# Linear attention and two dense layers on one core: two sums per slot accumulated on a bank copy, weight conversions in pairs

## The chip, the core and the metric

The kernel runs on one core of a Trainium2 chip. The metric is device time in microseconds (us). A core has a matrix engine (TensorE: PE in the rows, PEld for its weight loads), VectorE (DVE), ScalarE (ACT), GpSimd (POOL) and SyncE (SP, which here only issues transfers). Each engine works through its own instructions in order and waits for the others on semaphores. TensorE writes to PSUM, eight banks of 512 fp32 per partition; transfers run on 16 DMA engines.

## The reference

```python
kv = np.einsum('bhsd,bhse->bhde', k, v)          # attention: 8 x 8 heads, 576 tokens, 64 wide
out = np.einsum('bhsd,bhde->bhse', q, kv)
out = out / sqrt(mean(out * out) + 1e-06) * g_norm
x = out as [4608 tokens, 512]
h = x @ w_in;  g = max(h, 0) ** 2;  x = g @ w_out        # layer A: 512 -> 2048 -> 512
h = x @ w_in2; g = h * cos(h);      out = g @ w_out2     # layer B: the same sizes
```

The weights come as 64-bit floats. The kernel takes them as pairs of 32-bit words and makes fp32 of them with bit operations ("conversion"). Every large product is computed three times with a high and a low part of each operand (high·high, high·low, low·high), so that the sum has more bits than one pass gives.

## The kernel before

Up to about 498 us the kernel computes the attention, the first eight of layer A's 16 weight chunks, and converts weights. The rest, where the change lies, runs in 30 **slots**, made by `slots`: slot k is (layer m, token tile t, group q). Layer A (m = 0) has its other eight chunks left, two groups of four, for each of five token tiles (slots 0 to 9), layer B (m = 1) has four (slots 10 to 29). Tiles have halves of 512 tokens (t = 0, 1, 2) or 384 (t = 3, 4).

In a slot both matrix products are cut into 2 x 2 blocks, and the seven-product form of a 2 x 2 block product is used. The **first product** (`first_product`, L510) makes F0 to F6, 12 matmuls each, 84 a slot, into the bank pairs FA and FB by turns, in the order 0, 1, 3, 2, 5, 4, 6. Several of them accumulate on the one before in the same pair: F3 on F0, and so on. ScalarE and VectorE empty a pair in between: `keep` (L524, ScalarE, tiles m and u) copies F0 to SBUF, `add` (L530 for layer B, L534 for layer A, VectorE) adds F1 and the kept F0 to give block (0,0) of h, `last` (L539, ScalarE) takes F6. The four blocks of h then go through relu² (ScalarE, L543 and L547) or through h·cos h (`cos_1` to `cos_5`, L551 to L569, by turns ScalarE, VectorE, ScalarE, ScalarE, VectorE).

The **second product** of the slot runs 1.25 slots later (`LAG2`), between the matmuls of the first product of the next slots. In 25 slots (`seven`) it has the same form: `s_block` makes each of seven operands as a high part (ScalarE, L648, gh) and a low part (VectorE, L649, gl), some of them from differences of blocks (L631); `second_product` (L672) makes S0 to S6 into the pairs SA and SB by turns in the order `S_ORDER` = 0, 2, 3, 4, 5, 1, 6. `drain_product` adds each to sums in SBUF: on VectorE (L700), by a ScalarE copy to a tile `part` (L697) and a DMA that accumulates (L698), or by a ScalarE copy where it is the first (L692). The other five slots (q = 1 of layer A) use a plain product (`second`, L609; drained by VectorE, L622).

`run_slots` writes both products' matmuls in a fixed interleaving: one first-product matmul per step, 84 steps a slot, and the second product's spread evenly over the slot. Around them the list `jobs` sets when loads, copies and conversions are written, at a position in slots (`pos`; PH is a seventh of a slot). Weights for a product are loaded 2.7 sevenths ahead on SP's queue. A scheduler then orders each engine's instructions from this, so what stands in a queue is shown below from the built program.

While slots 1 to 7 run, the weights of layer B are converted: 16 units (`pair`), each a load of two 256 KB pieces into `raw`, the word operations (`words`, `value`, L119 to L133), four sums (L177), the high part (L189, ScalarE) and the low part (L191, VectorE), and two stores to `wi_d`. `raw` comes from the pool `conv` of two 4 KB buffers per partition, which the tiles `part` share later; the temporaries e and w come from the pool `t`, four of 2 KB.

## Time and profile before

| | us |
|---|---|
| median of 3 runs | 1583.31 (1581.37 to 1585.13) |
| the profiled execution | 1582.0 |
| its span on the core | 1580.2 |

The profile is that of one execution, 1.8 us longer than its span. TensorE's granted clock was 1.0 of full speed in every stretch. The share of the chain of work that ended last is PE 79%, DVE 8%, DMA 7%. Busy time of matmuls is modelled at their ends, so consecutive matmuls overlap in the rows: what one costs in a row of many is the distance between two starts, not its duration. Idle time of an engine that nobody waits for costs nothing.

### The profile page before, as it was taken

What the parts mean: (1) busy time and instruction counts of PE and PEld (TensorE: products, weight loads), DVE (VectorE), ACT (ScalarE), POOL (GpSimd) and SP (SyncE); (2) the same over time, 40 slices, a digit from 0 to 9 for tenths busy, and PEclk for the clock granted to TensorE, in tenths of its full rate; (3) what the DMA queues carried; (4) which work ended last, traced back from release to release, by engine and by line L of the source; (5) the groups of instructions that cost most, each with busy time, mean ns of one, the idle gap of its engine ahead of it and who ended that gap; (6) DMA issues with size and microseconds to landing.
All of it is one profiled execution on the core that took longest, in us unless ns stands there. A gap on an engine that the chain in (4) does not pass through costs nothing.

```text
span 1580.2 us, 24826 instructions
## 1 busy us (share of the span) xinstructions
PE 1547.6 (98%) x9164; PEld 1356.4 (86%) x9164; DVE 1256.6 (80%) x1714; ACT 1060.5 (67%) x1515; POOL 115.4 (7%) x125
## 2 busy tenths in 40 slices
PE   5999999999999999999999999999999999999998
PEld 3777777778887878888999899999999999999998
DVE  7988878788874888889847678967896788689777
ACT  5977777775443756565645667776777677777774
...
GB/s 317 282 158 243 263 235 278 240 202 207 185 219 256 298 271 336 302 335 330 374 281 291 246 213 270 266 277 246 267 260 291 230 260 290 277 363 314 284 351 164
DMA packets 236999, 425.53 MB, mean 269 GB/s; under 512 B 18512, under 2 KB 155216, under 8 KB 236880
## 3 DMA queue, kind: packets, MB, share of 16 engines
...
## 4 chain that ended last, share of the span: by engine, by line
PE 79%; DVE 8%; DMA 7%; issue 3%; ACT 2%; SPq 1%; POOL 0%; DVEq 0%; POOLq 0%; ACTq 0%
PE FA L510 14%; PE FB L510 14%; PE SA L672 12%; PE SB L672 12%; PE acc L422 10%; PE l L385 9%; PE SB L609 2%; PE SA L609 2%; DMA wi_d<-raw 2%; DMA raw<-in_wB 2%; PE o L385 1%; DMA sum<-part 1%; PE ss L385 1%; DMA ws_d<-raw 1%; DVE gl L649 1%
## 5 line engine op out<-in xcount | busy, mean ns | idle before, releaser
L510 PE MATMUL FA<-xh,wi 128*128 128x512 f32 (+1 forms) x840 | 306.0, 370 | 1.9 <-issue 1.0
L510 PE MATMUL FB<-xh,wi 128*128 128x512 f32 (+1 forms) x840 | 305.4, 370 | 0.0
L672 PE MATMUL SB<-ws,gh 128*128 128x256 f32 x1008 | 237.9, 280 | 1.1 <-ACT u L524 0.7
L672 PE MATMUL SA<-ws,gh 128*128 128x256 f32 x1008 | 237.9, 280 | 0.0
L672 PEld LDWEIGHTS SB<-ws,gh 128*128 128x128 f32 x1008 | 186.0, 188 | 14.4 <-ACT u L524 1.0
L672 PEld LDWEIGHTS SA<-ws,gh 128*128 128x128 f32 x1008 | 186.2, 188 | 13.2
L510 PEld LDWEIGHTS FA<-xh,wi 128*128 128x128 f32 x840 | 157.7, 188 | 12.1 <-issue 1.4
L510 PEld LDWEIGHTS FB<-xh,wi 128*128 128x128 f32 x840 | 157.8, 188 | 8.3 <-ACT h L539 0.3
L649 DVE TENSOR_TENSOR gl<-y,gh 128x1024 fp32r<-128x1024 f32 (+1 forms) x100 | 111.4, 1114 | 38.7 <-ACT gh L648 38.5
L672 PE MATMUL SA<-ws,gl 128*128 128x256 f32 x504 | 141.0, 280 | 1.1 <-DVE gl L649 1.1
L672 PE MATMUL SB<-ws,gl 128*128 128x256 f32 x504 | 141.2, 280 | 0.8 <-DVE gl L649 0.7
L698 POOL DMA_DIRECT2D sum<-part x71 | 60.3, 850 | 1093.4 <-ACT part L697 1078.6
L569 DVE SCALAR_TENSOR_TENSOR y<-y,h 128x1024 f32<-128x1024 f32 (+1 forms) x80 | 89.1, 1114 | 53.5 <-ACT y L565 53.2
L551 ACT ACTIVATE y<-h,zerob 128x1024 int32<-128x1024 f32 (+1 forms) x80 | 85.1, 1064 | 50.5 <-DVE h L530 50.5
L422 PE MATMUL acc<-gh,wh 128*128 128x512 f32 x288 | 113.6, 395 | 0.0
L422 PE MATMUL acc<-gl,wh 128*128 128x512 f32 x288 | 112.9, 392 | 0.0
L422 PE MATMUL acc<-gh,wl 128*128 128x512 f32 x288 | 112.6, 391 | 0.0
L510 PE MATMUL FA<-xl,wi 128*128 128x512 f32 (+1 forms) x300 | 111.0, 370 | 0.0
L510 PE MATMUL FB<-xl,wi 128*128 128x512 f32 (+1 forms) x300 | 110.9, 370 | 0.0
L672 PEld LDWEIGHTS SB<-ws,gl 128*128 128x128 f32 x504 | 94.7, 188 | 7.9 <-DVE gl L649 1.5
L672 PEld LDWEIGHTS SA<-ws,gl 128*128 128x128 f32 x504 | 94.7, 188 | 7.9 <-DVE gl L649 1.3
L385 PE MATMUL l<-xh,wh 128*128 128x512 f32 x240 | 96.6, 403 | 2.1 <-ACT xh L354 1.2
...
## 6 DMA issues: line engine op xcount, KB each, us to landing
wi<-wi_d SPq DMA_DIRECT2D x210, 512.0 KB, 7.0
ws<-ws_d SPq DMA_DIRECT2D x175, 512.0 KB, 5.9
sum<-part POOLq DMA_DIRECT2D x45, 512.0 KB, 7.6
kvld<-in_kv SPq DMA_DIRECT2D x32, 512.0 KB, 6.8
wi_d<-wh SPq DMA_DIRECT2D x24, 448.0 KB, 4.3
wi_d<-raw SPq DMA_DIRECT2D x24, 448.0 KB, 4.7
raw<-in_wA SPq DMA_DIRECT2D x20, 512.0 KB, 6.4
wo<-wo_d SPq DMA_DIRECT2D x20, 512.0 KB, 8.2
```

The source lines that it names most:

```text
L385: nc.tensor.matmul(ps, a[:, 0, cs], m[:], start=(c == 0 and k == 0), stop=(c == NKC - 1 and k == 2))
L422: nc.tensor.matmul(o, a[:, cs], m[:], start=(f == 0 and n == 0), stop=(f == NH - 1 and n == 2), skip_group_check=True)
L510: nc.tensor.matmul(ps[:, pp, :], a, b, start=(i in (0, 1, 2) and n == 0), stop=(n == 5), skip_group_check=True)
L551: nc.scalar.activation(out=y.bitcast(I32), in_=hs[k, b], func=AF.Identity, bias=zerob)
L569: nc.vector.scalar_tensor_tensor(out=y, in0=y, scalar=-2.0 * math.pi, in1=hs.pop((k, b)), op0=ALU.add, op1=ALU.mult)
L609: nc.tensor.matmul(ps, lhs, rhs, start=(a == 0 and (x, y) == (0, 0)), stop=last, skip_group_check=True)
L649: nc.vector.tensor_tensor(out=l, in0=src, in1=as32(h), op=ALU.subtract)
L672: nc.tensor.matmul(ps[:, b, :], lhs, rhs, start=(i in (0, 1, 2) and n == 0 and (m == 0 or b % 2 == 0)), stop=(n == 5), skip_group_check=True,)
L698: nc.gpsimd.dma_start(out=e, in_=part, accum_op=ALU.add)
```

## The change

**F0 and F1.** In 27 of the 30 slots (`seeded`: not 0, 1 and 10) ScalarE no longer copies F0 to SBUF. It copies it to the other bank pair of PSUM (`seed`), and F1's matmuls accumulate on the copy, so that the bank then holds F0 + F1; a ScalarE copy (`whole`, in layer A with the relu in it) takes it out, where VectorE added before. F1's first matmul now waits for the copy, so `run_slots` writes F1 late: its 12 matmuls come in the last 3 of its 12 steps (`HOLD` = 9), and in the first 9 the second product's run alone.

**S0 and S1.** In 22 slots (`seeded_s`) the same is done with S0 and S1; S1 is therefore made second (`S_ORDER` = 0, 1, 3, 2, 5, 4, 6), also where nothing is seeded, as in the last slot. VectorE's sum of S0 goes, and S1 is held back as F1 is.

**Conversions.** Layer B's weights are converted in eight double units (`pairs`) instead of 16: one `raw` of 8 KB (one buffer instead of two of 4 KB), two loads of 512 KB, every operation on twice the columns, high parts in two pieces. The temporaries become two of 4 KB, which `part` now shares instead of `raw`. Their positions run from 0.45 slots to 6.6 in steps of 0.88.

```diff
         elif kind == "pair":
-            raw = conv_p.tile([P, 4, P, 2], U32, tag="raw", name="raw")
+            raw = pools["raw"].tile([P, 4, P, 2], U32, tag="raw", name="raw")
...
+        elif kind == "pairs":
+            raw = pools["raw"].tile([P, 4, 2 * P, 2], U32, tag="raw", name="raw")
+            for df, dst in ((0, raw[:, 1:3]), (1, raw[:, 0::3])):
+                src = (wA, wB)[m][2 * f + df, :, 0, :].rearrange("p (k n) -> p k n", n=4 * P)
+                nc.sync.dma_start(out=dst.rearrange("p k n two -> p k (n two)"), in_=src)
...
-    S_ORDER = (0, 2, 3, 4, 5, 1, 6)
+    S_ORDER = (0, 1, 3, 2, 5, 4, 6)
     BY_DMA = (4, 5, 1, 6)
+    SEEDED = 2
+    def seeded(k):
+        return k >= SEEDED and TILES[slots[k][1]][1] <= TILES[slots[k - 1][1]][1]
+    def seeded_s(k):
+        return seeded(k) and k < len(slots) - 1
+    HOLD = 9
...
-                        ps[:, pp, :], a, b, start=(i in (0, 1, 2) and n == 0), stop=(n == 5), skip_group_check=True
+                        start=(n == 0 and (i in (0, 2) or i == 1 and not seeded(k))),
...
-    def last(k):
-        hs[k, (1, 0)] = h = t_tile(k, F32, "h")
+    def seed(k):
+        nc.scalar.copy(out=f_bank(k, 1), in_=f_bank(k, 0))
+
+    def whole(k, b, i):
+        hs[k, b] = h = t_tile(k, F32, "h")
         m = slots[k][0]
-        nc.scalar.activation(out=h, in_=f_bank(k, 6), func=AF.Copy if m else AF.Relu, scale=scale_of(k))
+        nc.scalar.activation(out=h, in_=f_bank(k, i), func=AF.Copy if m else AF.Relu, scale=scale_of(k))
...
+        if i == 0 and seeded_s(k):
+            nc.scalar.copy(out=blocks_of(t, s_bank(k, 1), m), in_=ps)
+            return
-        if q == 0 and m and i in (0, 2, 3, 6):
+        if q == 0 and m and i in (1 if seeded_s(k) else 0, 2, 3, 6):
...
-                part = blocks_of(t, conv_p.tile([P, 2, 512], F32, tag="raw", name="part"))
+                part = blocks_of(t, temp([P, 2, 512], F32, "part"))
...
-        (pairs_in(1, range(2 * NP)), pos(1), pos(7.6)),
...
+    late_stream = Stream(load_w, conv_w, [("pairs", 1, p, 0) for p in range(2 * NP)])
+    at(pos(0.15), late_stream.advance)
+    late_stream.place([pos(0.45 + 0.88 * k) for k in range(2 * NP)], 0)
...
-        at(pos(k + 1 * PH), keep, k, "m1", 0)
-        at(pos(k + 2 * PH), add, k, (0, 0), 1, "m1")
+        if not seeded(k):
+            at(pos(k + 1 * PH), keep, k, "m1", 0)
+            at(pos(k + 2 * PH), add, k, (0, 0), 1, "m1")
+        else:
+            at(pos(k + 1 * PH), seed, k)
+            at(pos(k + 2 * PH), whole, k, (0, 0), 1)
...
-    pools["t"] = ctx.enter_context(tc.tile_pool(name="t", bufs=4, side="left"))
+    pools["t"] = ctx.enter_context(tc.tile_pool(name="t", bufs=2, side="left"))
+    pools["raw"] = ctx.enter_context(tc.tile_pool(name="late", bufs=1, side="left"))
```

TensorE at the end of F0 in slot 12, before (FA takes F0, FB will take F1; SA is a second product under way):

```order
L510 MATMUL FA<-xh,wi 128x512
L672 MATMUL SA<-ws,gh 128x256 x2
L510 MATMUL FB<-xh,wi 128x512
L672 MATMUL SA<-ws,gl 128x256
L672 MATMUL SA<-ws,gh 128x256
L510 MATMUL FB<-xl,wi 128x512
```

The same place now:

```order
L529 MATMUL FA<-xh,wi 128x512
L698 MATMUL SA<-ws,gh 128x256 x2
L698 MATMUL SA<-ws,gl 128x256
L698 MATMUL SA<-ws,gh 128x256 x2
L698 MATMUL SA<-ws,gl 128x256
L698 MATMUL SA<-ws,gh 128x256 x2
L698 MATMUL SA<-ws,gl 128x256
L698 MATMUL SA<-ws,gh 128x256 x2
L698 MATMUL SA<-ws,gl 128x256
L698 MATMUL SA<-ws,gh 128x256 x2
```

F1 began two second-product matmuls after F0's last; now 20 stand between them (the ten after these rows read the same), and F1's matmuls then follow four at a time.

ScalarE around the copy of F0 of slot 4, a slot of layer A, before (m is that copy; e and wh are steps of a conversion, xh a split of the tile's input):

```order
L189 CAST wh<-raw 128x896
L575 CAST gh<-h 128x1024
L539 ACTIVATE h<-FB 128x1024
L120 ACTIVATE e<-e,expb 128x512
L547 ACTIVATE h<-h 128x1024
L478 CAST xh<-xraw 128x1024
L575 CAST gh<-h 128x1024
L478 CAST xh<-xraw 128x1024
L524 ACTIVATE m_7018<-FA 128x1024
```

And now, with the seed `FB<-FA`:

```order
L602 CAST gh<-h 128x1024
L566 ACTIVATE h<-FB 128x1024
L574 ACTIVATE h<-h 128x1024
L119 ACTIVATE e<-e,expb 128x1024
L561 COPY FB<-FA 128x1024
L199 CAST wh<-raw 128x768
```

Between the block taken from FB (F6 of the slot before) and the copy stood five instructions, and a cast wh two places ahead of them; now two stand there, one of them the step e of a conversion, and the cast wh comes behind the seed. In slots 3 and 5 a cast wh stands two places before the seed.

VectorE at the end of the program, where the last slot's operands are made, before (t and y are differences of blocks, sum the drains):

```order
L649 TENSOR_TENSOR gl<-t,gh 128x2x384
L631 TENSOR_TENSOR t<-y,t 128x2x384
L569 SCALAR_TENSOR_TENSOR y<-y,h 128x2x384
L700 TENSOR_TENSOR sum<-SB,sum 128x768
L649 TENSOR_TENSOR gl<-t,gh 128x2x384
L649 TENSOR_TENSOR gl<-y,gh 128x2x384
```

The same end now:

```order
L596 SCALAR_TENSOR_TENSOR y<-y,h 128x2x384
L675 TENSOR_TENSOR gl<-y,gh 128x2x384
L658 TENSOR_TENSOR t<-y 128x2x384
L658 TENSOR_TENSOR t<-y,t 128x2x384
L658 TENSOR_TENSOR y<-y 128x2x384
L729 TENSOR_TENSOR sum<-SA,sum 128x768
L675 TENSOR_TENSOR gl<-t,gh 128x2x384 x2
```

The last step of the cosine of block (1,0) (L569, now L596) stood after both differences t and after a low part; it now stands first, its low part follows at once because S1 needs it, and the differences t, their low parts and a drain of SA (S1's) come behind it.

## Rows read from the trace of the kernel before

**Rows 1.** The page: busy us, share of the span, instructions.
```profile
PE 1547.6 (98%) x9164; PEld 1356.4 (86%) x9164; DVE 1256.6 (80%) x1714; ACT 1060.5 (67%) x1515; POOL 115.4 (7%) x125
```

**Rows 2.** Stretches: length, busy us of PE, PEld, DVE, ACT, POOL; clock, DMA.
```profile
500.00:860.00 360.00, 358.02 (x1709) 311.08 (x1709) 290.14 (x358) 213.72 (x239) 0.00 (x0) 1.00 0.92 316
860.00:1340.00 480.00, 480.00 (x3070) 437.99 (x3069) 381.59 (x332) 345.32 (x355) 35.69 (x42) 1.00 0.86 258
1340.00:1553.60 213.60, 212.58 (x1510) 211.89 (x1509) 165.12 (x183) 159.17 (x207) 22.10 (x26) 1.00 0.99 316
1553.60:1580.20 26.60, 20.06 (x159) 19.08 (x157) 18.66 (x21) 11.38 (x15) 2.55 (x3) 1.00 0.41 105
```

**Rows 3.** Timeline of TensorE in slot 14: start, duration, instruction [idle before].
```profile
1000.19 0.39 PE L510 MATMUL FA<-xraw,wi 128*128 128x512 f32 x1
...
1000.65 0.40 PE L510 MATMUL FA<-xh,wi 128*128 128x512 f32 x1
```

**Rows 4.** Groups by line and shape: count, busy us, mean ns, idle before.
```profile
L524 ACT ACTIVATE m<-FA 128x1024 f32<-128x1024 f32 x18 | 18.4, 1022 | 3.2 <-PE FA L510 3.1
L524 ACT ACTIVATE m<-FA 128x768 f32<-128x768 f32 x12 | 9.7, 809 | 3.1 <-PE FA L510 3.1
L700 DVE TENSOR_TENSOR sum<-SB,sum 128x1024 f32<-128x1024 f32 x24 | 29.2, 1218 | 3.9 <-PE SB L672 3.9
```

**Rows 5.** Timeline of TensorE: last matmuls of products 0 and of one S.
```profile
638.67 0.39 PE L510 MATMUL FA<-xh,wi 128*128 128x512 f32 x1
...
922.26 0.40 PE L510 MATMUL FA<-xh,wi 128*128 128x512 f32 x1
...
1157.45 0.40 PE L510 MATMUL FA<-xh,wi 128*128 128x512 f32 x1
...
1436.68 0.28 PE L672 MATMUL SB<-ws,gh 128*128 128x256 f32 x1
```

**Rows 6.** Timeline of ScalarE: the copies that empty these banks.
```profile
640.95 0.95 ACT L189 CAST wh<-raw 128x896 fp32r<-128x896 f32 x1 [6.76 <-DMA wo<-wo_d]
...
648.18 1.02 ACT L524 ACTIVATE m<-FA 128x1024 f32<-128x1024 f32 x1
...
922.69 1.03 ACT L524 ACTIVATE m<-FA 128x1024 f32<-128x1024 f32 x1 [0.17 <-PE FA L510]
...
1161.11 1.02 ACT L524 ACTIVATE m<-FA 128x1024 f32<-128x1024 f32 x1
...
1439.92 0.80 ACT L697 COPY part<-SB 128x768 f32<-128x768 f32 x1
```

**Rows 7.** Timeline of TensorE at the end of the program.
```profile
1559.84 0.28 PE L672 MATMUL SA<-ws,gh 128*128 128x256 f32 x1
1561.18 0.39 PE L672 MATMUL SA<-ws,gl 128*128 128x256 f32 x1 [1.07 <-DVE gl L649]
...
1564.65 0.39 PE L672 MATMUL SB<-ws,gl 128*128 128x256 f32 x1 [0.46 <-DVE gl L649]
...
1574.95 0.28 PE L672 MATMUL SB<-ws,gh 128*128 128x256 f32 x1
```

**Rows 8.** Timeline of ScalarE there: h of F6.
```profile
1554.27 0.79 ACT L539 ACTIVATE h<-FB 128x768 f32<-128x768 f32 x1
```

**Rows 9.** Timeline of VectorE there: last cosine step of block (1,0).
```profile
1561.91 0.95 DVE L569 SCALAR_TENSOR_TENSOR y<-y,h 128x768 f32<-128x768 f32 x1
```

**Rows 10.** Groups by shape of VectorE, 500 to 860 us: one conversion unit.
```profile
L191 DVE TENSOR_TENSOR raw<-raw,wh 128x896 fp32r<-128x896 f32 x16 | 17.3, 1083 | 2.0 <-ACT wh L189 2.0
L177 DVE TENSOR_TENSOR raw<-raw 128x128 f32<-128x128 f32 x56 | 13.7, 284 | 0.3
...
L124 DVE SCALAR_TENSOR_TENSOR w<-raw,w 128x512 uint32<-128x512 uint32 x14 | 9.6, 685 | 0.1
...
L119 DVE TENSOR_SCALAR e<-raw 128x512 uint32<-128x512 uint32 x14 | 5.9, 423 | 13.4 <-DMA raw<-in_wB 13.4
```

**Rows 11.** The page, DMA issues: count, KB each, median us to landing.
```profile
wi<-wi_d SPq DMA_DIRECT2D x210, 512.0 KB, 7.0
...
wi_d<-raw SPq DMA_DIRECT2D x24, 448.0 KB, 4.7
```

More of the change, by code (lines that the diff above doesn't have):

```diff
@@ L144, in load_w @@
         elif kind == "pair":
-            raw = conv_p.tile([P, 4, P, 2], U32, tag="raw", name="raw")
+            raw = pools["raw"].tile([P, 4, P, 2], U32, tag="raw", name="raw")
             for df, dst in ((0, raw[:, 1:3]), (1, raw[:, 0::3])):
@@ L169, in conv_steps @@
         raw = raws.pop((kind, m, f, i))
-        if kind in ("pair", "seven"):
-            w, e = words(raw, [P, 4, P])
+        if kind in ("pair", "seven", "pairs"):
+            n = 2 * P if kind == "pairs" else P
+            w, e = words(raw, [P, 4, n])
             yield
-            a = as32(raw.rearrange("p a n two -> p (a n two)")).rearrange("p (o n) -> p o n", n=P)
+            a = as32(raw.rearrange("p a n two -> p (a n two)")).rearrange("p (o n) -> p o n", n=n)
             value(raw, a[:, 0:4], w, e)
@@ L177, in conv_steps @@
                 nc.vector.tensor_tensor(out=a[:, o], in0=a[:, x], in1=a[:, y], op=op)
-            where = [n for n in ("c", "x") if n in pools]
+            where = [p for p in ("c", "x") if p in pools]
             if where:
-                parts = [(0, 8, pools[where[0]].tile([P, 8, P], F32R, tag=where[0], name="wh"))]
+                size = 1024 // n
+                parts = [
+                    (o, o + size, pools[where[0]].tile([P, size, n], F32R, tag=where[0], name="wh"))
+                    for o in range(0, 8, size)
+                ]
             else:
-                parts = [(o, o + 4, temp([P, 4, P], F32R, "wh")) for o in (0, 4)]
+                parts = [(o, o + 4, temp([P, 4, n], F32R, "wh")) for o in (0, 4)]
             q, pp = divmod(f - first_pair[m], 2)
-            dst = (wi_d if kind == "pair" else ws_d)[m, q][:, :, :, pp, i, :]
+            dst = (ws_d if kind == "seven" else wi_d)[m, q][:, :, :, pp]
+            dst = dst.rearrange("p o x i n -> p o x (i n)") if kind == "pairs" else dst[:, :, :, i, :]
             l = a.bitcast(F32R)
@@ L675, in second_product @@
                         rhs,
-                        start=(i in (0, 1, 2) and n == 0 and (m == 0 or b % 2 == 0)),
+                        start=(n == 0 and (m == 0 or b % 2 == 0) and (i in (0, 2) or i == 1 and not seeded_s(k))),
                         stop=(n == 5),
@@ L733, in place @@
             for k, (n, item) in enumerate(zip(positions, self.items)):
-                steps = (0, 0.06, 0.13, 0.3, 0.45)
+                steps = (0, 0.07, 0.15, 0.22, 0.3, 0.4, 0.62)
                 if n < nA0:
@@ L865, in run_slots, with held @@
         ]
-        seconds = [k + LAG2 + n / size[k] for k in range(len(slots)) for n in range(size[k])]
+        def held(x):
+            return 2 * PH - (2 * PH - x) * (12 - HOLD) / 12 if PH <= x < 2 * PH else x
+        seconds = [
+            k + LAG2 + (held(n / size[k]) if slots[k][0::2] in seven and seeded_s(k) else n / size[k])
+            for k in range(len(slots))
+            for n in range(size[k])
+        ]
         firsts = [(k, i) for k in range(len(slots)) for i in ORDER]
@@ L875, in run_slots @@
         nf, ns = 12 * len(firsts), 0
-        n = 0
-        while n < nf or ns < len(seconds):
+        due = []
+        for n in range(nf):
+            k, j = divmod(n, 84)
+            if seeded(k) and 12 <= j < 24:
+                j = 24 - (24 - j) * (12 - HOLD) / 12
+            due.append(k * 84 + j)
+        n = done1 = 0
+        while done1 < nf or ns < len(seconds):
             here = n / 84
@@ L883, in run_slots @@
                 ns += 1
-            if n < nf:
+            while done1 < nf and due[done1] <= n:
                 next(steps1)
+                done1 += 1
             n += 1
@@ L907 @@
         right("pad", 1).tile([P, 56], F32, name="pad")
+        pools["raw"] = right("conv", 2)
         x_p, g_p, ev_p, pools["t"] = (right(n, b) for n, b in (("x", XB), ("g", 3), ("ev", 2), ("tmp", 8)))
```

17 lines of the change are left out of this document (10 added, 7 removed).

## The prediction

> **What bounds the kernel now.** I read the page's busy times first, then the stretches, then single timelines. TensorE is busy for 1547.6 of 1580.2 us [rows 1]. That share is an average over a start, the slots and an end, so the stretches matter: in 860 to 1340 us TensorE has no idle time at all (480.00 of 480.00), in 500 to 860 it lacks 1.98 us, in 1340 to 1553.6 it lacks 1.02, and in the last 26.6 us 6.54 [rows 2]. Busy times of matmuls overlap, so I checked the distance of starts: one 512-column matmul of F and the two 256-column matmuls of S behind it take 1000.65 - 1000.19 = 0.46 us [rows 3], and at the end S matmuls alone start every (1574.95 - 1564.65) / 88 = 0.117 us [rows 7] (16 left of S3 and four products of 18). So F costs 0.23 and S 0.117, alone or mixed. A 512-token slot of layer B is then 84 x 0.46 = 39 us of matmuls. Nothing in the change removes a matmul or makes one shorter. All that can be gained in the slots is 1.98 + 1.02 us, and in the end part of its idle time; everything before 500 us keeps its order. What can be lost is each wait that the seeds put on TensorE's queue.
>
> **VectorE's load.** Of 360 us it works 290 (81%) in 500 to 860, where layer A's slots and the conversions meet [rows 2]. A unit there costs 2 x 0.42 + 3 x 0.69 + 4 x 0.28 + 1.08 = 5.1 us [rows 10], two units 10.2. A double unit has the same ten kinds of step on twice the columns. No row shows those widths for word operations; by doubling each the cost stays 10.2, by the fp32 step on 1024 columns (1.22 [rows 4], 0.13 less than twice 0.69) and a like saving on the short ones it is about 9. I take 9: eight times 1.2, so 10 us (0 to 10). Eight additions of F0 and four sums of S0 go too, at 1.22 or about 0.95 us: another 13. VectorE loses about 23 of 290 us there, and in layer B some 33 instructions or 36 us of 547. This hides behind TensorE except where TensorE waited for it, so its worth is at most the idle time above: I take -2.5 us (0 to -3.0).
>
> **The seeds of F, 27 places.** What a seed must beat: F0's last matmul starts, lasts 0.39 us, the copy starts 0.03 later and takes about 1.02 (0.81 with 384 tokens) [rows 4 to 6]; a wake-up adds under 0.1. That is 1.5 us (1.25). No row shows a ScalarE copy that writes PSUM; I bound its price by half and by twice these copies to SBUF, and take them as they are (at twice, a punctual seed would just fit in large tiles and cost 0.2 us in small ones). TensorE has meanwhile, by the order, 0.23 us and 20 S matmuls at 0.117: 2.6 us; in small tiles 0.175 and 15: 1.9. So a punctual seed costs nothing, with 1.1 (0.65) us to spare. The question is how punctual ScalarE is. Its copies of F0 before are the nearest measure: in the 27 slots, 14 begin within 0.1 us of the matmul's end, as at 922.69 after 922.26 + 0.40; three come 0.4 to 0.7 late; seven of layer B 1.1 to 3.4 late, as at 1161.11 after 1157.85 in slot 18; and those of slots 2, 4 and 6 are 8.7 to 9.6 late, as at 648.18 after 639.06 [rows 5, 6]. Nobody noticed, for F1 went to the other bank.
>
> In layer B, with each lateness kept and set against its own hold (24 to 29 matmuls stand in slots 14, 18, 22 and 26), the excess is 0.0, 1.1, 1.7, 0.2, 0.6, 0.4, 1.6 and 1.0 for slots 11, 14, 18, 22, 24, 25, 26 and 28, in all 6.6 us. But the new order puts fewer instructions between the slot's start and the copy in those slots: I take 2.0 (0 to 6.6).
>
> In layer A the slots 2, 4 and 6 would wait 7.2, 8.3 and 7.9 us by the old lateness, together 23.4. Its cause is in the rows: ScalarE stood 6.76 us in front of the cast wh of a conversion, up to 640.95, with four to eight microseconds of work queued behind it [rows 6]. The new order has this cast behind the seed in slots 2, 4 and 6, but before it in 3 and 5, and a step e, which needs a load, before it in 4; VectorE, which makes ScalarE late there, has 8% less to do. I take 2.5 us, one wait of some microseconds or two short ones (0 to 23.4).
>
> The Trainium skill ("ScalarE: Activation LUTs", section "Step-by-step: what each stage is for") says that ScalarE writes to PSUM sooner than to SBUF. No run here shows it. Were a seed 0.1 us shorter by it, the exposed ones, some 15, would give back 1.5 us, and the sum would be 1587.8.
>
> **The seeds of S, 22 places.** The copy needs 0.28 + 0.03 + 1.0 + 0.1 = 1.4 us (1.2 in small tiles); TensorE has 0.117 and nine F matmuls: 2.2 (1.7). Spare: 0.8 (0.5). The nearest measure is ScalarE's copies of SA and SB to `part`, 71 of them: 42 within 0.1 us, the latest 2.96 after its matmul, 1439.92 against 1436.96 [rows 5, 6]. The excess over the spare is 0.13 us a copy in large tiles and 0.39 in small ones: 13 and 9 seeds give 5.2. ScalarE gets 33 more instructions in layer B, over 4% of the time there, and stands at 72 to 75% [rows 2]. What queues behind a late seed is ScalarE's next casts, so lateness is passed on. I take 2.0 (0 to 5.2).
>
> **The end.** Here S_ORDER matters although the last slot has no S seed. S1 needs block (1,0) of y, which is made last. It stood sixth; it now stands second, where TensorE comes at 1559.84 [rows 7]. The block's chain begins with h at 1554.27 and ended its cosine at 1561.91 + 0.95 [rows 8, 9], with other work between; the high and low part add 0.8 and 0.95. In the new order two casts and two differences leave the chain: I take its low part for ready at 1563.6 (1561.4 if its eight steps ran without a gap, 1564.7 as before). S1's 17 other matmuls end at 1565.9. VectorE's next instruction is the drain of S1, which waits for that end; the low part of S3's operand stands behind it, so S3 goes on at 1565.9 + 0.87 + 0.95 = 1567.8. Before, S3 went on at 1564.65 [rows 7], after idle times of 1.07 and 0.46 us and smaller ones, and as many matmuls follow. The end moves by +3.1 us (0.9 to 4.2).
>
> **What costs nothing.** The single `raw` makes the next load wait on SP's queue for the store's landing, 4.7 us [rows 11], and loads of wi stand behind it. Those are issued 2.7 products of 5.6 us ahead and land in 7.0 [rows 11], so 8 us are to spare; without them each late wi would hold F for the difference. `part` shares two temporaries with the conversions, but those are done by slot 7 and the first `part` comes in slot 10.
>
> **Sum.** On the profiled execution's own 1582.0 us (span and 1.8): -2.5 + 2.0 + 2.5 + 2.0 + 3.1 = +7.1, 1589 us. The median of the three runs is 1.3 above that execution; I don't add this, the range covers it.
>
> **Rivals.**
> 1. The holds do their work: every seed is punctual, the end's +3.1 and the -2.5 cancel, 1582 to 1584. For it: 14 of 27 copies were punctual to 0.1 us. Against it: ten were over 1 us late. It decides where ScalarE is within 1.1 us in nearly all slots.
> 2. ScalarE is as late as before in layer A: 23.4 + 6.6 + 5.2 + 3.1 = 38 us, less what a standing TensorE lets the others catch up, so 1605 to 1615. For it: the three rows' cause, conversion steps on both queues, is still there. Against it: the new order and the smaller load.
> 3. Faster: VectorE's lighter queue gives back all of the 3.0 us in the slots, and the same relief runs the end's chain dense, so that S1 and S3 wait no longer than S2 and S3 did. 1582.0 - 3.0 - 2 = 1577. Price and point: it needs block (1,0)'s low part by about 1560, while its eight steps from 1554.27 add up to 7.1 us, so F6 itself must end earlier; and no seed may be late.
>
> **Chances.** Runs of this kernel spread by 0.24%, so 0.2% (3.2 us, 1580.1 to 1586.5) is about what counts as no change. Forecast, +3.2 to +20 us: 0.55. Rival 1: 0.27. Rival 2: 0.08. Rival 3: 0.10. Faster 0.10, same 0.27, slower 0.63. The range leaves out rival 2 and the better half of rival 3: 1578 to 1603; the forecast's own is 1586 to 1597.
>
> **What would show it.** Right: F's bank copies in layer B within a microsecond and a half of F0's end; TensorE's idle time in 860 to 1553.6 up from 1.0 to 3 to 8 us, put down to the copies of ScalarE; in the last 27 us one idle time of 2 to 5 us in front of S1's second matmul and one of 1 to 2 in front of S3's, with the last matmul at 1578 or later by the old clock. VectorE's busy time about 60 us lower, ScalarE's 30 higher. Wrong: TensorE's idle time between 500 and 1553 under 2 us (rival 1, or 3 with a short end), or single waits over 5 us in front of F1 in layer A (rival 2). A different matmul pace in the holds would break the sum itself.

## The result, and the profile after

The changed kernel takes 1598.9 us (median), the kernel before 1582.6 in the same runs: ratio 1.0096, 95% interval 1.0076 to 1.0116, so some 15 us slower. One of the four runs of the change, at 1762.8 us and a granted clock of 0.82, is left out of the ratio. The forecast was 1589, 7 us slower. The direction holds, and so does the whole range (1578 to 1603), but not the forecast's own, 1586 to 1597: the loss is twice the forecast. The profiled execution has a span of 1597.8 us, 17.6 more than before. Its page, busy us of the engines [rows 1]:

```profile
PE 1555.0 (97%) x9164; PEld 1360.7 (85%) x9164; DVE 1204.1 (75%) x1597; ACT 1090.0 (68%) x1544; POOL 112.1 (7%) x121
```

VectorE works 52 us less, ScalarE 30 more, as forecast (60 and 30). Where the time went is read best from fixed points of TensorE's order, which exist in both kernels: F0's first matmul of a slot, F's last matmul, the last matmul of all. TensorE's timeline before (start, duration, instruction), at slots 0 and 10 and the two ends:

```profile
499.30 0.47 PE L510 MATMUL FA<-xh,wi 128*128 128x512 f32 x1 [1.02 <-issue]
...
842.33 0.39 PE L510 MATMUL FA<-xh,wi 128*128 128x512 f32 x1
...
1553.33 0.34 PE L510 MATMUL FB<-xh,wi 128*128 128x384 f32 x1
...
1575.31 0.28 PE L672 MATMUL SB<-ws,gh 128*128 128x256 f32 x1
```

and after:

```profile
499.68 0.47 PE L529 MATMUL FA<-xh,wi 128*128 128x512 f32 x1 [1.60 <-issue]
...
849.11 0.39 PE L529 MATMUL FA<-xh,wi 128*128 128x512 f32 x1
...
1564.88 0.34 PE L529 MATMUL FB<-xh,wi 128*128 128x384 f32 x1
...
1592.97 0.28 PE L698 MATMUL SB<-ws,gh 128*128 128x256 f32 x1
```

The differences of the four starts are 0.4, 6.8, 11.6 and 17.7 us. So layer A's slots lose 6.4 us, layer B's 4.8, and the tail behind F's last matmul 6.1. The first and the last of the stretches of [rows 2] show the same (length, busy us of PE, PEld, DVE, ACT, POOL; clock; DMA share, GB/s):

```profile
500.00:860.00 360.00, 351.91 (x1677) 305.24 (x1676) 275.32 (x287) 208.92 (x231) 0.00 (x0) 1.00 0.89 314
...
1553.60:1597.80 44.20, 35.31 (x241) 33.87 (x239) 28.99 (x32) 18.25 (x24) 2.55 (x3) 0.88 0.45 131
```

TensorE's idle time grew from 2.0 to 8.1 us in the first stretch, where least was forecast, and its granted clock fell at the end. What it waited for from 480 us on (sum, times, longest, us):

```profile
PE SA L698 <- ACT gh L674: 3.7, 2, 2.8
PE SB L698 <- ACT SB L717: 2.7, 3, 1.9
PE FB L529 <- ACT u L548: 2.2, 1, 2.2
PE FA L529 <- ACT m L548: 1.7, 1, 1.7
...
PE FB L529 <- ACT FB L561: 0.5, 1, 0.5
```

The seeds of F (L561) cost one wait of half a microsecond in 27 slots. The long waits are of other kinds, and the three largest follow.

**Slot 1, which has no seed.** The timeline of both engines there:

```profile
541.71 0.83 ACT L199 CAST wh<-raw 128x768 fp32r<-128x768 f32 x1 [5.56 <-DVE raw L132]
542.44 1.02 ACT L548 ACTIVATE u<-FB 128x1024 f32<-128x1024 f32 x1
...
543.51 0.50 PE L529 MATMUL FB<-xh,wi 128*128 128x512 f32 x1 [2.16 <-ACT u L548]
```

ScalarE stands 5.56 us in front of the high-part cast of a double unit, which waits for VectorE. Behind it stands the copy u that empties FB, and TensorE stands 2.16 us for that.

**Slot 23, a seed of S.** Here three engines hand on one delay:

```profile
1363.58 1.01 ACT L726 COPY part<-SB 128x1024 f32<-128x1024 f32 x1 [3.02 <-DMA sum<-part]
...
1365.35 0.96 DVE L675 TENSOR_TENSOR gl<-y,gh 128x768 fp32r<-128x768 f32 x1 [3.81 <-ACT gh L674]
...
1368.28 0.83 ACT L674 CAST gh<-t 128x768 fp32r<-128x768 f32 x1 [2.25 <-DVE t L658]
1369.02 0.79 ACT L717 COPY SB<-SA 128x768 f32<-128x768 f32 x1
...
1369.86 0.39 PE L698 MATMUL SB<-ws,gh 128*128 128x256 f32 x1 [1.90 <-ACT SB L717]
```

Both part buffers are in use, so ScalarE waits 3.02 us for an accumulating DMA to free one. The cast behind it is late for VectorE, VectorE's difference t is late for ScalarE, the seed stands behind that cast, and S1 waits 1.90 us.

**The end.** TensorE in the last slot, S1 second:

```profile
1574.22 0.58 PE L698 MATMUL SA<-ws,gh 128*128 128x256 f32 x1 [2.78 <-ACT gh L674]
1575.21 0.58 PE L698 MATMUL SA<-ws,gl 128*128 128x256 f32 x1 [0.41 <-DVE gl L675]
...
1578.80 0.41 PE L698 MATMUL SA<-ws,gh 128*128 128x256 f32 x1
...
1580.31 0.55 PE L698 MATMUL SA<-ws,gh 128*128 128x256 f32 x1 [0.88 <-ACT gh L674]
```

and the clock (sixth value behind the length) around it:

```profile
1573.00:1574.00 1.00, 0.00 (x0) 0.00 (x0) 0.31 (x1) 0.66 (x1) 0.00 (x0) 0.95 1.06 206
1574.00:1575.00 1.00, 0.58 (x1) 0.29 (x1) 0.80 (x1) 0.17 (x1) 0.00 (x0) 0.50 0.25 43
...
1584.00:1585.00 1.00, 1.00 (x10) 1.00 (x9) 0.22 (x1) 0.00 (x0) 0.00 (x0) 0.93 0.00 0
```

The forecast waits are there, in front of S1 (of its first matmul, which needs the high part, and only 0.41 us of its second) and of S3. What the forecast did not have: during the idle 2.78 us the granted clock falls to 0.5, the lower level of 1.2 GHz, and stays for some 10 us. S1's matmuls then come every 0.22 us (16 steps from 1575.21 to 1578.80) instead of 0.117 [rows 7].

### The profile page after: what moved, and what is told of

It is laid out like the page before. It is cut to its first block, busy times and chain, and to the rows that moved or that the text cites. A ratio compares the mean times of both kernels' runs of the same rounds, so it can differ in the third digit from the quotient of the medians.

```text
span 1597.8 us, 24731 instructions
## 1 busy us (share of the span) xinstructions
PE 1555.0 (97%) x9164; PEld 1360.7 (85%) x9164; DVE 1204.1 (75%) x1597; ACT 1090.0 (68%) x1544; POOL 112.1 (7%) x121
## 4 chain that ended last, share of the span: by engine, by line
PE 79%; DVE 7%; DMA 7%; ACT 3%; issue 3%; SPq 1%; DVEq 0%; ACTq 0%; POOLq 0%
PE FB L529 13%; PE FA L529 13%; PE SA L698 12%; PE SB L698 12%; PE acc L432 10%; PE l L395 9%; PE SA L636 3%; PE SB L636 3%; DMA sum<-part 2%; DMA raw<-in_wB 1%; PE o L395 1%; DMA ws_d<-raw 1%; PE ss L395 1%; DMA wi_d<-raw 1%; DVE sum L729 1%
## 5 line engine op out<-in xcount | busy, mean ns | idle before, releaser
L529 PE MATMUL FA<-xh,wi 128*128 128x512 f32 (+1 forms) x840 | 299.6, 370 | 3.3 <-ACT m L548 1.7
L529 PE MATMUL FB<-xh,wi 128*128 128x512 f32 (+1 forms) x840 | 299.3, 371 | 2.7 <-ACT u L548 2.2
L698 PE MATMUL SA<-ws,gh 128*128 128x256 f32 x1008 | 231.0, 283 | 3.7 <-ACT gh L674 3.7
L698 PE MATMUL SB<-ws,gh 128*128 128x256 f32 x1008 | 229.9, 282 | 2.7 <-ACT SB L717 2.7
L698 PEld LDWEIGHTS SA<-ws,gh 128*128 128x128 f32 x1008 | 182.5, 190 | 15.5 <-ACT gh L674 4.1
L698 PEld LDWEIGHTS SB<-ws,gh 128*128 128x128 f32 x1008 | 181.5, 190 | 14.6 <-ACT SB L717 4.0
L596 DVE SCALAR_TENSOR_TENSOR y<-y,h 128x1024 f32<-128x1024 f32 (+1 forms) x80 | 89.3, 1116 | 107.8 <-ACT y L592 107.6
L727 POOL DMA_DIRECT2D sum<-part x67 | 56.9, 850 | 1108.5 <-ACT part L726 543.5
L674 ACT CAST gh<-y 128x1024 fp32r<-128x1024 f32 (+1 forms) x100 | 94.9, 960 | 14.3 <-DVE y L596 7.6
```

Source lines behind the costliest of these rows:

```text
L529: nc.tensor.matmul(ps[:, pp, :], a, b, start=(n == 0 and (i in (0, 2) or i == 1 and not seeded(k))), stop=(n == 5), skip_group_check=True,)
L596: nc.vector.scalar_tensor_tensor(out=y, in0=y, scalar=-2.0 * math.pi, in1=hs.pop((k, b)), op0=ALU.add, op1=ALU.mult)
L674: nc.scalar.copy(out=h, in_=src)
L698: nc.tensor.matmul(ps[:, b, :], lhs, rhs, start=(n == 0 and (m == 0 or b % 2 == 0) and (i in (0, 2) or i == 1 and not seeded_s(k))), stop= ...
L727: nc.gpsimd.dma_start(out=e, in_=part, accum_op=ALU.add)
```

## The experiments

Theory A, from these traces: the conversions and the end carry the loss, and S's seeds most of the rest; F's seeds are free. The rival is the forecast's own account, in which the conversions bring 2.5 us. All runs in one table: ratio to the kernel before by time, and what the profiled run lost against before, by the fixed points above (up to slot 0; slots 0 to 9, layer A; slots 10 to 29, layer B; the tail). The last column has the time, in whole us, for which TensorE's granted clock stood at 0.5 from slot 0 on, and where; in the kernel before it never did.

| run | ratio (95%) | to slot 0 | A | B | tail | clock at 0.5 |
|---|---|---|---|---|---|---|
| the change | 1.0096 (1.0076–1.0116) | 0.4 | 6.4 | 4.8 | 6.1 | 10 tail |
| e1 single units, all seeds | 1.0113 (1.0096–1.0130) | 0.8 | 3.4 | 8.5 | 4.6 | 3 B, 3 tail |
| e2 double units alone | 1.0026 (1.0016–1.0035) | 1.7 | 3.8 | 0.8 | 0.0 | 3 A |
| e3 change, old last slot | 1.0081 (1.0066–1.0096) | 1.2 | 4.8 | 7.3 | -0.1 | 3 A |
| e4 change, filled wait | 1.0111 (1.0092–1.0130) | 0.8 | 6.0 | 5.6 | 3.4 | 3 A |
| e5 F's seeds alone | 1.0050 (1.0032–1.0067) | -0.9 | 3.0 | 5.0 | 0.1 | 3 A |
| e6 S's seeds alone | 1.0038 (1.0024–1.0052) | 3.4 | 0.5 | 9.2 | -0.1 | none |
| e7 double units later | 1.0041 (1.0024–1.0058) | 0.1 | 6.5 | -1.8 | 0.0 | 3 A |
| e8 F's seeds, no hold | one run, 1594.7 us | 1.5 | 3.2 | 8.0 | 0.0 | 3 A |
| e9 change, third part buffer | 1.0090 (1.0068–1.0111) | 2.6 | 4.9 | 1.1 | 5.2 | 3 A, 7 tail |
| e10 single units, bunched | 1.0053 (1.0038–1.0068) | 0.4 | 8.8 | -0.6 | 0.0 | 3 A |
| e11 e3 and e9 together | 1.0045 (1.0028–1.0062) | 1.9 | 4.9 | 1.0 | -0.1 | none |
| e12 e11, uneven places | 1.0049 (1.0036–1.0063) | 0.4 | 6.1 | 1.1 | -0.1 | 7 A |
| e13 double units late | 1.0076 (1.0062–1.0090) | 3.0 | 13.0 | 1.5 | 0.0 | 17 A |
| e14 e11, late places | 1.0086 (1.0073–1.0100) | 0.7 | 12.9 | 2.0 | -0.1 | 14 A |
| e15 e11, no unit in slot 1 | 1.0044 (1.0032–1.0056) | 3.2 | 4.9 | 4.1 | -0.1 | 7 A |
| e16 e15 without S's seeds | 1.0033 (1.0021–1.0045) | 0.8 | 2.1 | 3.7 | 0.0 | 3 A, 3 B |
| e17 double units, close places | 1.0068 (1.0055–1.0081) | 3.2 | 7.9 | -0.6 | 0.0 | 7 A |
| e18 e11, close places | 1.0062 (1.0049–1.0076) | -0.2 | 7.3 | 1.1 | -0.1 | 7 A |

The change, e3 and e4 have the same order in layer B and lost 4.8, 7.3 and 5.6 there; the change, e3, e4, e9 and e11 the same in layer A, and lost 4.8 to 6.4; the column up to slot 0 varies by itself. So a difference under 2.5 us of a whole layer in one profile says nothing here, and the times resolve nothing smaller. Single slots repeat better: slot 12 takes 39.36 us in all five. A profile is one execution, not always a middle one: e6's took 1594.9 us (median 1588.6), e13's 1599.5 (1594.4) and e15's 1594.0 (1589.6), so their columns add up to more than their ratios.

What the time at 0.5 costs differs. In layer A the change, e3, e9 and e11 are the same, and TensorE waits 2.14 to 2.16 us in slot 1. Slot 1 lost 4.8 us in the change and in e11, where the clock stayed at 1.0, and 6.3 and 6.5 in e3 and e9, where it then stood at 0.5 for 3 us; but over slots 1 and 2 together all four lost 4.2 to 4.4. In part the slower matmuls stood in for waits of 0.6 us for VectorE and 0.3 to 0.4 for ScalarE, which the change and e11 have there and e3 and e9 do not. In layer B nothing gave it back: slot 23 lost 3.9 us in e1, where the clock fell behind a wait of 2.17 us, and 2.3 in e3, where it did not behind 2.04.

### Each part by itself

**e1**, all seeds, conversions as before:

```diff
...
-    late_stream = Stream(load_w, conv_w, [("pairs", 1, p, 0) for p in range(2 * NP)])
...
+        (pairs_in(1, range(2 * NP)), pos(1), pos(7.6)),
```

> The changed kernel with layer B's weights converted as before (16 single units, two raw buffers of 4 KB, part in them), all seeds kept. Theory A (the double units, not the seeds, cost the time in slots 0 and 1: a high-part cast of a double unit waits for VectorE in ScalarE's queue in front of the copy that empties FB): the 5.8 us lost there go, ratio to the kernel before about 1.006 (1591 to 1594), and the single slots 2 to 6 show no loss. Theory B (the forecast's: the pairs relieve VectorE and bring 2.5 us, the seeds cost it): slower than the changed kernel, 1599 to 1602.

**e2**, the reverse:

```diff
...
-    SEEDED = 2
+    SEEDED = 99
...
-    S_ORDER = (0, 1, 3, 2, 5, 4, 6)
+    S_ORDER = (0, 2, 3, 4, 5, 1, 6)
...
```

> The kernel before with the double units alone: no seed, old order of S products, no hold. Theory A: slots 0 and 1 lose about 5.8 us as in the changed kernel, and nothing else changes: ratio 1.003 to 1.004 (1587 to 1590). Theory B: 1 to 3 us faster than before, ratio 0.998 to 0.9995.

e2 falls to theory A: the double units alone cost 0.26%, 4 us, where the forecast had a gain. The place is slot 1 again:

```profile
541.99 0.83 ACT L199 CAST wh<-raw 128x768 fp32r<-128x768 f32 x1 [4.43 <-DVE raw L132]
...
543.80 0.80 PE L529 MATMUL FB<-xh,wi 128*128 128x512 f32 x1 [2.14 <-ACT u L548]
```

e1 contradicts theory A in the sum: without the double units the kernel is no faster (1.0113 against 1.0096, intervals overlap). It loses 3 us less in layer A, but still 3.4, and 3.7 more in layer B. One of its waits in layer A is again a conversion, VectorE waiting for a load (0.43 us of work, 3.26 of waiting) with a drain behind it that TensorE needs:

```profile
588.48 0.43 DVE L119 TENSOR_SCALAR e<-raw 128x512 uint32<-128x512 uint32 x1 [3.26 <-DMA raw<-in_wB]
...
590.10 0.50 PE L637 MATMUL SB<-gh,wo 128*128 128x512 f32 x1 [1.83 <-DVE sum L650]
```

So the parts do not add. That what one part delays the other would have had to wait for anyway is a reading that no run tests; some 1.6 us of e1's loss in layer B are the clock (slot 23 above), which did not fall there in the change.

**e5**, F's seeds alone (single units, and of the S products all as before):

```diff
...
     def seeded_s(k):
-        return seeded(k) and k < len(slots) - 1
+        return False
...
-    S_ORDER = (0, 1, 3, 2, 5, 4, 6)
+    S_ORDER = (0, 2, 3, 4, 5, 1, 6)
```

> The kernel before with F's seeds and hold alone: single units, no seed of S, the old order of S products everywhere. Theory A (the seeds of F stand beside S matmuls and cost no wait; the loss of layer B comes from S's seeds): in slots 10 to 29 at most 0.5 us lost and no pace of +0.16 us a slot, the end as before, in layer A -1 to +3 us; ratio 0.9995 to 1.002 (1582 to 1586). Theory B (the forecast's: 4.5 us for F's seeds, 2.0 of them in layer B): ratio 1.003 (1587 to 1589).

**e6**, S's seeds alone (single units, the last slot as before; `seeded_s` gets the condition of `seeded` written out, so that it holds in the same slots as in the change):

```diff
...
-    SEEDED = 2
+    SEEDED = 99
...
-        return seeded(k) and k < len(slots) - 1
+        return k >= 2 and TILES[slots[k][1]][1] <= TILES[slots[k - 1][1]][1] and k < len(slots) - 1
...
```

> The kernel before with S's seeds, S1 second and the hold of S1 alone: single units, no seed of F, the last slot in the old order. Theory A: the +0.16 us a slot of layer B is here (3 us by slot 29), and so are the waits in front of S1 in slots 23 and 27 (2 us each); with little in layer A the ratio is 1.003 to 1.005 (1588 to 1591). Theory B (S's seeds cost 2.0 us by ScalarE's lateness alone, the pace being F's): ratio 1.0013.

e6 came out by time where theory A put it (1.0038), though without the two waits of 2 us in front of S1: TensorE waited for its seeds 1.9 us in four times. Theory A held too little against F's seeds: 0.5% by e5, where it had at most 0.2%. TensorE's waits for them in e5's layer B are small (0.6 us in two); the larger one is a part copy:

```profile
PE SB L700 <- ACT part L728: 2.5, 2, 1.6
```

The rest is pace, which neither account had in the right place. In undisturbed slots the change loses 0.16 us a slot (39.36 instead of 39.20 us), e5 0.08, e6 0.09, e2 0.00. In the change one step in slot 14 shows it, the first F1 matmul behind the run of S:

```profile
1010.90 0.50 PE L529 MATMUL FB<-xh,wi 128*128 128x512 f32 x1
1011.23 0.40 PE L529 MATMUL FB<-xl,wi 128*128 128x512 f32 x1
```

0.33 us instead of 0.23 [rows 3]; why is not shown. In all it is some 2.6 us: by e9 below, where nothing else is lost in layer B, 1.1 and the 1.6 that it wins in slot 26.

**e8**, e5 without the hold:

```diff
-    HOLD = 9
+    HOLD = 0
```

F1's first matmul is written ahead of the copy here, and the copy overwrites its share.

> F's seeds alone as in the run with F's seeds only, but without the hold: F1's matmuls come evenly behind F0's, 0.46 us after it, so the whole copy shows as a wait. Theory A (a punctual seed needs 1.4 us from F0's last start, 1.2 in small tiles, of which the hold covers all): about 1.0 us in front of F1 in each of the 27 seeded slots, 0.7 in small tiles, more where ScalarE is late: 20 to 40 us more than with the hold. If a copy into PSUM took half or twice the 1.02 us of a copy to SBUF, 0.5 or 2.0 us each: 8 or 50 us.

A clear miss: 1594.7 us in its one run against 1589.6, 5 us and not 20 to 40. TensorE and ScalarE in slot 12:

```profile
927.37 0.40 PE L530 MATMUL FB<-xh,wi 128*128 128x512 f32 x1
...
928.80 1.01 ACT L562 COPY FB<-FA 128x1024 f32<-128x1024 f32 x1
...
929.86 0.50 PE L530 MATMUL FB<-xl,wi 128*128 128x512 f32 x1
```

Between the two F1 matmuls TensorE ran 18 of S (927.60 to 929.62). The kernel writes one F1 matmul per step here, so it was the scheduler that put them there; the hold says mostly what it does by itself. The price of an uncovered seed is therefore still not measured.

### The end

**e3**, the last slot in the old order:

```diff
+    def s_order(k):
+        return (0, 2, 3, 4, 5, 1, 6) if k == len(slots) - 1 else S_ORDER
```

> The changed kernel with the old order of S products (0, 2, 3, 4, 5, 1, 6) in the last slot alone. Theory A (S1 second waits 2.8 us for its operand, TensorE's granted clock falls to 0.5 in that wait and stays there for some 10 us; so the end costs 6.1 us, 3 by waits and 3 by the clock): no half clock at the end, F's last matmul to S's last 22 to 23 us as before instead of 28.4, ratio about 1.006 (1591 to 1594). Theory B (the clock falls in any case, by less work towards the end): clock 0.5 again, and only 3 us gained, ratio 1.0075.

**e4**, the order as changed, but TensorE kept at work in the wait:

```diff
+        if k == len(slots) - 1 and i == 1:
+            for _ in range(22):
+                nc.tensor.matmul(
+                    psum["FA"][:, 0, : 2 * P],
...
```

> The changed kernel with 22 more matmuls (256 columns, into FA, which nobody reads any more) in front of S1 in the last slot, where TensorE stands for 2.8 us. Theory A: the clock stays at 1.0, the matmuls of S1, S3 and S2 come every 0.12 us instead of 0.21, and although 2.6 us of work are added the end is 2.5 to 3 us shorter than in the changed kernel: ratio about 1.0078 (1595 to 1597). Theory B (the operands of VectorE set the pace there, the clock only fills time that is lost anyway): no change, 1597 to 1600, or slower by the matmuls added, to 1602.

The clock of e3 at the same place:

```profile
1574.00:1578.00 4.00, 2.85 (x19) 2.48 (x20) 4.00 (x6) 3.12 (x5) 0.00 (x0) 1.00 0.52 98
```

The fill in TensorE's timeline of e4, and the clock behind it:

```profile
1572.04 2.80 PE L694 MATMUL FA<-ws,gh 128*128 128x256 f32 x22
```

```profile
1574.00:1578.00 4.00, 3.25 (x26) 2.85 (x24) 3.07 (x5) 1.01 (x2) 0.00 (x0) 1.00 0.26 49
```

In both the clock stays at 1.0. e3's tail is as long as before (-0.1): the order in one slot was the whole 6.1 us. By time e3 can't be told from the change (1.0081 and 1.0096), but e9 and e11 below, which differ in this order alone, can be told apart (1.0090 and 1.0045). e4's tail is 2.7 us shorter than the change's, though 22 matmuls were added; so of the 6.1 us some 3.4 are the waits and some 2.7 the clock. By time e4 can't be told from the change (1.0111); this split rests on the traces.

Two more runs have this end without the fill, with the same wait of 2.78 us, and the clock's part varies in them: in e9 the clock stood at 0.5 for 7 us and the tail lost 5.2, in e1 for 3 us and 4.6. Above the 3.4 of e4 that is 1.8 and 1.2 us. There the clock fell only after the wait had ended, in e9 more than 2 us after (S1's first matmul came at 1571.3):

```profile
1574.00:1575.00 1.00, 1.00 (x6) 0.87 (x5) 0.96 (x2) 0.87 (x2) 0.00 (x0) 0.50 0.00 0
```

### The part buffers

**e9**, every third part in the raw that lies unused after slot 7:

```diff
...
-                part = blocks_of(t, temp([P, 2, 512], F32, "part"))
+                n_part[0] += 1
+                if n_part[0] % 3:
+                    part = blocks_of(t, temp([P, 2, 512], F32, "part"))
+                else:
+                    part = blocks_of(t, pools["raw"].tile([P, 4, 2 * P], F32, tag="raw", name="part")
...
```

> The changed kernel with a third buffer for the tiles part (every third one lies in the conversions' raw, which nobody uses after slot 7). In the changed kernel ScalarE stood 3.02 us in front of a part copy for a DMA to free the buffer, and the seed of S behind it came 1.9 us late in slot 23. Theory D (the late seeds of layer B stand behind part copies that wait for a buffer): the waits of ScalarE for DMA sum<-part in 860 to 1553 us fall from 7.4 to under 2 us, the loss of slots 22 to 29 falls by 2 to 3 us, ratio 1.0080. Theory E (ScalarE is late by its own load and by VectorE's differences t): the waits for the DMA go, the seeds are as late, no change in time, ratio 1.0096.

The part copies of layer B in the change and in e9 (count, busy, mean ns, idle before and what ended it):

```profile
L726 ACT COPY part<-SB 128x1024 f32<-128x1024 f32 x22 | 22.2, 1009 | 14.5 <-PE SB L698 9.6 <-DMA sum<-part 4.8
```

```profile
L731 ACT COPY part<-SB 128x1024 f32<-128x1024 f32 x22 | 22.1, 1007 | 9.7 <-PE SB L699 9.6
```

The waits for the DMA are gone (4.8 of 14.5 us in this group), and the view of waits lists none of TensorE from 860 to 1553 us any more, those for the seeds of S included. Layer B's loss is 1.1 us instead of 4.8 to 7.3: theory D. ScalarE was not late by its load; it stood for a buffer. The later runs with all seeds and three buffers lost 1.0 to 2.0 us there, except e15: 4.1, with one wait of 1.4 us for a cast whose cause stays open. By time e9 alone can't be told from the change.

**e11** joins e3 and e9:

> The changed kernel with the old order of S products in the last slot and the third part buffer. If both act by themselves the gains add: 6 us at the end and 0 to 3 us in slots 22 to 29, 1589 to 1592, ratio 1.004 to 1.006; still slower than before, by the losses of slots 0 to 6 and the 0.16 us a slot of layer B. If the third buffer brings nothing: as the run with the old order alone, 1595, ratio 1.008.

1.0045, clear of the intervals of e3 and of e9: each of the two shows by time beside the other, and half of the change's loss is gone. Most of what is left is layer A.

### The place of the conversions

From here on it is the list of places at which conversions are written that changes, as in **e7** (double units alone):

```diff
...
-    late_stream.place([pos(0.45 + 0.88 * k) for k in range(2 * NP)], 0)
+    late_stream.place([pos(0.7 + 0.85 * k) for k in range(2 * NP)], 0)
```

> The double units alone, as in the run with the pairs only, but written 0.25 slots later (from 0.7 slots in steps of 0.85), so that in ScalarE's order the two casts of the high part stand behind the copies u and m of slot 1 and no longer in front of them. Theory A (the cast that waits for VectorE holds up the copy that frees FB): the 2.1 us in front of F of slot 1 go, 3 to 4 us in all, ratio 0.9995 to 1.0005. Rival C (the double units delay slot 1 by VectorE's own queue, or by their loads, wherever the casts stand): the loss stays, ratio 1.0025.

e7 missed (1.0041): the wait for u is gone, and other waits of the same kind have come, for casts and low parts in slots 1 to 3 and 6. Theory A named the right mechanism and too narrow a place.

**e10**, the kernel before with its units in twos:

```diff
...
-        (pairs_in(1, range(2 * NP)), pos(1), pos(7.6)),
...
+    late_stream = Stream(load_w, conv_w, pairs_in(1, range(2 * NP)))
+    late_stream.place([pos(0.45 + 0.88 * (k // 2)) for k in range(4 * NP)], 0)
```

> The kernel before with its single units and two raw buffers, but two units written together at each of the eight places at which the double units were written in the changed kernel. Theory F (the double units cost by where they are written, ten microseconds of conversion steps at a time, not by their width or the single buffer): slots 0 to 6 lose 4 to 6 us as with the double units, ratio 1.0025 to 1.004. Theory G (the longer instructions or the one raw buffer make the loss): at most 1 us lost, ratio 1.000.

e10 decides between theories F and G: single units with two buffers, bunched, lose 0.53%, no less than the double ones. ScalarE and TensorE in slot 1:

```profile
541.73 1.78 ACT L200 CAST wh<-raw 128x896 fp32r<-128x896 f32 x2 [4.40 <-DVE raw L183]
...
544.48 0.77 PE L530 MATMUL FB<-xh,wi 128*128 128x512 f32 x1 [3.14 <-ACT u L549]
```

Neither the width nor the one buffer is needed for the loss: ten microseconds of steps written at once where VectorE has no idle time make it. That such places exist is in the trace of before (DVE is the third value):

```profile
540.00:560.00 20.00, 19.77 (x88) 16.07 (x87) 19.69 (x25) 10.98 (x12) 0.00 (x0) 1.00 0.82 278
...
600.00:640.00 40.00, 39.70 (x175) 32.58 (x174) 39.97 (x46) 22.44 (x23) 0.00 (x0) 1.00 0.97 343
```

**e12** on e11, then **e13** (double units alone) and **e14** (on e11):

```diff
...
+    late_stream.place([pos(x) for x in (0.25, 1.65, 2.5, 3.4, 4.25, 5.4, 6.2, 7.0)], 0)
+    late_stream.place([pos(x) for x in (3.4, 4.25, 5.4, 6.2, 7.0, 7.8, 8.6, 9.4)], 0)
```

> The changed kernel with the three causes met together: the last slot in the old order of S products, a third part buffer, and the eight double units written where VectorE had idle time before (0.25, 1.65, 2.5, 3.4, 4.25, 5.4, 6.2 and 7.0 slots instead of 0.45 to 6.6 in even steps). Theory F (the conversions cost by their place): the 5 us of slots 0 and 1 and the 1.6 of slot 6 go, and with what the seeds bring in slots 2 to 5 and 26 (-2.2 and -1.6) against 3 us of pace the kernel is level with the kernel before or just ahead, 1580 to 1584, ratio 0.998 to 1.001. If the places bring nothing: as the run with last slot and parts, ratio 1.0045.

> The double units alone (no seeds, old orders), written at 3.4, 4.25, 5.4, 6.2, 7.0, 7.8, 8.6 and 9.4 slots: none in slots 0 to 2, where VectorE is busy without a gap for tens of microseconds. Theory F (the conversions cost by their place): slots 0 to 2 lose under 1 us against 5.3 with the even places, whole kernel ratio 0.998 to 1.0005 (1579 to 1583). Theory G (the double width or the one raw buffer costs): the 4 us stay, in later slots, ratio 1.0025.

> The changed kernel with the last slot in the old order, the third part buffer, and the double units at the same late places. Theory F: the 7 us of slots 0 to 2 go and the rest stays (3 us of pace in layer B, less 1.6 in slot 26 and what the seeds bring in slots 3 to 5): ratio 0.998 to 1.001. Theory G: ratio 1.0035 to 1.005.

e12 missed: its unit at 1.65 slots met VectorE's backlog. e13 and e14 agree with the theory up to slot 8 and miss in the sum: with no unit before slot 3.4 they stood 2.8 and 2.9 us better against before at slot 8 than at slot 0, and then lost 16 us in slots 8 and 9, where the last units came. There TensorE waited for m, behind a conversion's cast, 3.9 us in e13 and 4.8 in e14, which the rows show:

```profile
844.21 0.83 ACT L199 CAST wh<-raw 128x768 fp32r<-128x768 f32 x1
...
845.81 0.69 PE L534 MATMUL FA<-xh,wi 128*128 128x384 f32 x1 [4.78 <-ACT m L553]
```

It also waited for weights (3.5 and 2.1 us, `ws<-ws_d`), and why these were late is not known. The clock took a part as well. In e13 it stood at 0.5 from 840 to 853 us; TensorE was busy for 7.9 of these 13 us, 4.88 of the first ten, so the clock's part of the 16 us is at most half of that, an estimate of 4:

```profile
840.00:850.00 10.00, 4.88 (x14) 4.41 (x15) 9.93 (x13) 4.50 (x6) 0.00 (x0) 0.50 0.93 367
```

**e15** on e11, **e16** on e15 without S's seeds; **e17** (double units and the third buffer) and **e18** (on e11):

```diff
...
+    late_stream.place([pos(x) for x in (0.25, 2.1, 2.8, 3.5, 4.25, 5.4, 6.2, 7.0)], 0)
+    late_stream.place([pos(x) for x in (0.25, 2.1, 3.2, 3.75, 4.3, 5.4, 6.1, 6.8)], 0)
```

> The changed kernel with the last slot in the old order, the third part buffer, and the double units at 0.25, 2.1, 2.8, 3.5, 4.25, 5.4, 6.2 and 7.0 slots: none in slot 1, none after 7.4. Theory F (place alone): nothing lost in slots 1 and 2, under 1 us in 3 and 6 and none in 8 and 9, 1580 to 1583, ratio 0.998 to 1.0005. If units at 2.1 to 3.5 meet the same full VectorE in the next token tile's slots: 2 to 4 us lost there, ratio 1.002.

> As the run before it, but with F's seeds alone, S products in the old order everywhere. Theory F with the pace of S's holds (0.09 us a slot): 1.6 us faster than the run before it, 1579 to 1582, ratio 0.997 to 0.9995. If S's seeds relieve VectorE enough to pay for their pace: the same or slower than the run before it.

> The double units alone (no seeds, old orders of products), with the third part buffer and the units at 0.25, 2.1, 3.2, 3.75, 4.3, 5.4, 6.1 and 6.8 slots, the next load written 0.45 slots behind a unit's first step instead of 0.62. Theory F: no loss in slots 0 to 9 beyond 1 us and the 2 to 3 us that the runs with late places stood better at slot 8, no wait for a part buffer in slot 26 (1.6 us): 1578 to 1581, ratio 0.997 to 0.9995. Rival: with so close a spacing the one raw buffer is late, and casts wait for it: 2 to 5 us lost, ratio 1.002.

> The changed kernel with the last slot in the old order, the third part buffer and the same places. Theory F: as the run before it plus 3 us of pace in layer B from the two holds: 1581 to 1584, ratio 0.999 to 1.001. If the seeds save VectorE and ScalarE waits that the run before it has: equal to it.

All four missed: level with the kernel before, or ahead of it, was expected. In all four slots 1 and 2 lose nothing, and slot 3 (about 595 to 640 us) loses 4.1 to 7.4 us. In or behind its waits the clock stood at 0.5 for 3 us in e16 and e18 and for 7 in e15 and e17, so part of the loss may be the clock's. The wait is of the known kind; in e17:

```profile
640.55 0.83 ACT L199 CAST wh<-raw 128x768 fp32r<-128x768 f32 x1 [5.11 <-DVE raw L132]
...
642.38 0.79 PE L637 MATMUL SB<-gh,wo 128*128 128x512 f32 x1 [4.50 <-ACT gh L603]
```

The rival there, a late load into the one raw buffer, does not fit this wait: VectorE was busy for all of 625 to 640 us (15.00 of 15).

No run found eight places for units of nine microseconds that are all free, and no version is faster than the kernel before. Whether such places exist stays open; so does whether sixteen single units, with all the rest mended, would do.

## Why the prediction was wrong

- **The step that failed: VectorE's load, -2.5 us.** The double unit is as cheap as taken (2 x 0.69 + 3 x 1.22 + 4 x 0.42 + 0.95 + 1.22 = 8.9 us, forecast 9) and VectorE's busy time fell. The conclusion failed. I set eight savings of 1.2 us against VectorE's mean load of 81% over 360 us, but in 540 to 560 and 600 to 640 it works without a gap, and a lump of nine microseconds there delays ScalarE's casts and all that stands behind them. Alone it costs 4 us (e2), 6.6 from the term; e10 shows that the lump does it without the wider steps. In the sum layer A's slots stood at about 0 (-2.5 and +2.5) and lost 6.4 us. Beside the seeds the units' price does not show by time (e1 is no faster than the change).
- **The end, +3.1 us: right place, half the size.** Waits in front of S1 and S3 came as worked out and cost some 3.4 (e4). The other 2.7 are the clock (1.2 in e1 and 1.8 in e9), which this sum did not have.
- **Seeds of F in layer B, +2.0 us.** There are no waits for them in the change; punctual in 18 of 27 slots, the late ones covered. 0.08 us a slot of pace stands in the term's place, half of the 2.6 us.
- **Seeds of F in layer A, +2.5 us.** One wait of 0.5 us. Rival 2, ScalarE as late as before, did not come: the cast in front of the seed is the danger, as it said, but it struck the copies u and m of slots 0 and 1 instead, which I had not looked at because no seed stands there.
- **Seeds of S, +2.0 us.** 2.7 us of waits, the size about right, by a wrong cause: not ScalarE's load but a part buffer (e9). That the size came out is luck. The forecast dismissed `part` because the conversions are over by slot 10; it did not ask whether two buffers are enough for the parts themselves.
- **Price of a copy into PSUM.** Taken as that of a copy to SBUF. Measured, seeds and m copies of the change:

```profile
L561 ACT COPY FB<-FA 128x1024 f32<-128x1024 f32 x7 | 7.0, 1003 | 2.8 <-PE FA L529 2.8
...
L548 ACT ACTIVATE m<-FA 128x1024 f32<-128x1024 f32 x11 | 11.2, 1022 | 1.9 <-PE FA L529 1.9
```

The Trainium skill ("ScalarE: Activation LUTs", section "Step-by-step: what each stage is for") has ScalarE write to PSUM sooner than to SBUF. The trace agrees in the sign, by 0.02 us against m; against the part copies to SBUF (1009 ns above), which are the same operation as the seed, by 0.006. Either is too little to move the sum; the 1.5 us that the forecast worked out for it are not there.

- **Signs and slips.** TensorE's idle time in 860 to 1553.6 us rose from 1.0 to 2.7 us, short of the 3 to 8 named. The sign that would break the sum itself, another pace of matmuls in the holds, came: 0.16 us a slot. One step of the working is off: twice 0.69 less 1.22 is 0.16, not 0.13; the 9 us do not hang on it. The direction came true in part by luck, since the lumps and the clock, which brought much of the loss, were not in the sum.
